# Five engines' orders, the PSUM banks, the load queues and the engines of copies dealt anew in a fused linear-attention and MLP kernel

## The chip, the cores and the metric

The kernel runs on one core of one Trainium2 chip. The metric is device time in microseconds (us), the median over several runs; lower is better. A run's time holds the span that the profile shows and some 3 us around it. The engines are PE (matmul; PEld is its weight load), DVE (VectorE), ACT (ScalarE), POOL (GpSimd) and SP, which here only issues transfers.

## The reference

```python
B, H, S, D = 4, 8, 768, 48                     # r, k, v, w: (B, H, S, D), f32
for t in range(S):                              # per batch and head, state (D, D)
    y[t] = r[t] @ (state + (u * k[t]) v[t]^T)
    state = w[t][:, None] * state + k[t] v[t]^T
x = y as (B*S, H*D) = (3072, 384)
h = x @ w_in                                    # (384, 1024)
solu = h * softmax(h)
ln = (solu - mean) / sqrt(var + 1e-6) * g_ln
out = ln @ w_out                                # (1024, 384)
```

## The kernel before

The sequence is cut into six chunks of 128 rows; with four batches that makes 24 units, `units = [(c, b) ...]`, of 128 rows and 384 columns each. Units of one batch follow each other through a state; units of different batches are free. Each unit goes through these stages, whose short names are the words of the order:

- Loads `LW LK LR LV` of w, k, r and v, 192 KB each, into rings of seven buffers (`NIO`). Weights come as `LI0..2` (w_in, 512 KB each), `LO0, LO1` (w_out, 768 KB each), `LU` and `LG`.
- Decays: `lw` (ACT, logarithm of w), `cum` (PE, running sums), `ex` (ACT, exponential in PSUM), `kp` (DVE, scaled k and r).
- Scores: `krk`, `krr` (PE transposes) with `kr` (a copy out of PSUM), or `kt` (a DMA transpose on SP in their place); `M` (PE) and `m` (masked copy, mostly DVE).
- The bonus of u: `p`, `q` (POOL products), `dg` (DVE sum), `vb` (v as bf16), `dv` (POOL).
- `Y` (PE, the output y) with `y` (copy), `S` (PE) with `et` (ACT) and `st` (DVE) for the next state. With `Y.i` the bonus is added by a matmul with the identity and `y` is a plain copy on ACT; with `Y.n`, `y` adds it on DVE.
- The MLP, transposed: `X` (PE) with `xT` (copy), `H` (PE, 24 matmuls of 128 columns, needs all of w_in), `e` (ACT, exp), `he` (DVE, product), `hq` (ACT, square), `ea` (POOL, halves the matmuls of a row sum), `Oa`, `Ob` (PE), `qm` (DVE), `lv`, `rs` (ACT), `o` (scaled copy) and `out` (store, through a ring of four buffers).
- Once: `wi` (cast of w_in), `gw` (w_out times gain), `mn` (PE column mean), `mc` (its copy, ACT), `ce` (centring of w_out), `hot` (warm-up matmuls on a tile of zeros; `hotN` has N of them).

No scheduler decides the order. A string, `ORDER`, lists some 900 words; each names a stage, a unit and, behind the dot, a choice. For PE words the choice is the PSUM bank, for copies the engine (`a` ACT, `d` DVE, `p` POOL), for loads and stores the queue:

```python
queue = {"": sp, "a": act, "g": pool}
...
for word in ORDER.split():
    word, _, how = word.partition(".")
    name = word.rstrip("0123456789")
    stages[name](int(word[len(name):]), how)
```

A wrapper, `InOrder`, keeps each engine's instructions in the order of the words, and SP's and ACT's transfers in one common order. An engine's queue is in order: an instruction that waits holds all behind it, a transfer's issue included. A transfer on SP or ACT also waits until the transfer eight places before it in the common order has landed, as both share eight semaphores in turn.

All of an engine's instructions come through the wrapper, so the profile gives nearly all of them the same line (L86), and groups are told apart by tile names: `ps` is any PSUM bank, `kr_in` the buffer of k and r, `w` (written `w<-`) the scaled w_out, `he`, `e`, `hq`, `o`, `y`, `st`, `et`, `xT`, `kr`, `kp`, `lw`, `vb`, `dv`, `dg` as above. ACTq and SPq rows are those engines' transfer issues.

Of the kernel before, what the change touches and what calls it, by code (L numbers as in the profile page):

```python
# [31 lines left out]
xT4.d ce1.d LK9 H2.6 hq0.a he1 e3 he3 LW12 e2 krk7.5 Oa0.2 he2 krr7 hq1.a cum10.3 LV8.g Ob0 ex10 Oa1.0 LR9 hq3.a
LV7 p8 cum8.6 LW13 Ob1 LW14 LK11 ex8 q7 vb6.p dg5 kr7.d kp10 lw11 qm0 Oa3.5 lv0 qm1 lv1 LV10.g p10 q8 rs0 M7.3
dg7 rs1 dv5 o0.a out0 vb7.p kp8 lw12 hq2.a Ob3 cum11.6 krk10.2 o1.d H4.0 m7.d Y5.n4 LR12.g dv7 Oa2.3 krr10 qm3
out1 p9 dg6 dg8 ex11 vb8.a dv6 q9 kp11 lv3 cum9.6 e4 rs3 Ob2 y5.d LV9 o3.a he4 ex9 kp9 lw14 kr10.a S7.5 LK12
Y6.n1 qm2 y6.d lv2 krk8.4 Y7.n0 krk11.6 krr8 y7.d S8.7 X5.2 et7 st7 krr11 lw13 rs2 LW17 o2.a et8 cum12.0 LR14.g
xT5.a ex12 q10 kr8.d S6.5 kr11.d hq4.a krk9.2 vb11.p out3 LK14 out2 M8.3 LK13 LR15.g LR17.g krr9 st8 kp12 LK17
et6 kr9.d H5.6 X6.0 m8.a M10.1 st6 e5 xT6.d M9.3 p11 Oa4.5 m10.d LW15 he5 q11 LR13.g X7.0 kt12 cum14.1 m9.a xT7.a
dv8 M11.3 ex14 m11.d sel8 Ob4 vb9.p kp14 LK15 hq5.a cum13.6 LW18 lw17 qm4 S11.0 ex13 Oa5.4 sel9 lv4 lw15 cum17.1
dg9 rs4 LR18.g kp13 Y8.n3 Ob5 ex17 cum15.6 y8.d dv9 o4.a Y9.n3 out4 LV12.g kp17 LV15.g et11 qm5 kt14 S9.5 st11  # L40
ex15 lv5 vb10.a y9.d H6.1 rs5 et9 LV14.g o5.a e6 st9 LV13.g kp15 p12 p13 dg11 he6 dg10 X8.3 X9.0 xT8.a H7.4 out5
q12 xT9.a e7 lw18 hq6.a H8.6 dv11 e8 M12.0 LV16.g he7 H9.2 m12.d LK18 Oa6.5 he8 dg12 e9 vb12.a S10.4 kt15 he9
hq7.a Ob6 hq8.a dv10 LW16 qm6 lv6 rs6 p14 LR16.g et10 Y11.n1 S12.0 et12 Oa7.6 o6.a LK16 y11.d lw16 Y10.n7 st10
Ob7 kt13 y10.d M14.3 st12 vb15.a LK20 M15.1 q13 vb13.a hq9.a qm7 m14.d m15.d lv7 dv12 rs7 Y12.n5 o7.a Oa8.0 y12.d
cum16.3 X11.7 Ob8 cum18.1 out6 p15 ex16 X12.5 xT11.d q14 q15 LR19.g qm8 kp16 vb16.a lv8 H11.6 rs8 o8.a ex18
xT12.d H12.4 LR20.g LW21 vb14.p dg13 LW19 dg15 e11 Oa9.0 p16 kp18 out7 e12 X10.1 dv15 he11 Ob9 xT10.a ea11.p he12
q16 lw21 hq11.a out8 qm9 lv9 M13.1 S15.3 et15 rs9 m13.d ea12.p cum21.4 ex21 o9.d H10.6 LK21 LR21 LW20 Oa11.0
LV18.g st15 kp21 lw19 cum19.1 e10 Ob11 Y15.n4 he10 hq12.a LK19 p18 kt16 S13.3 dv13 Y13.n5 S16.6 qm11 ex19 y15.d
lv11 out9 ea10.p kp19 LV22 LW22 rs11 et13 y13.d o11.a LK22 Oa12.7 out11 LV19.g lw20 M16.0 dg14 st13 vb18.a hq10.a
et16 m16.d p17 X15.4 Ob12 dv14 X13.3 p19 Y14.n2 xT15.d LR22 S14.5 xT13.d qm12 lv12 LV17.g rs12 st16 o12.a et14  # L50
kt17 y14.d q17 cum20.0 H13.3 dg16 H15.6 q18 ex20 st14 out12 e13 e15 vb19.a q19 kp20 he13 kt18 dv16 X14.2 xT14.d
Oa10.5 LV23 hq13.a Y16.n0 Ob10 dg17 he15 ea13.p qm10 lw22 vb17.a H14.1 ea15.p lv10 dv17 LW23 M17.6 y16.d kt19
dg18 rs10 Oa13.0 o10.a m17.d out10 cum22.3 X16.5 Ob13 e14 xT16.a Y17.n7 he14 qm13 dv18 kt20 p20 M18.5 vb23.p
y17.d hq15.a m18.d LV20.g ex22 kp22 H16.1 p21 LR23 Oa15.7 Y18.n6 dg19 dv19 LK23 q20 ea14.p p22 Ob15 X17.4 vb22.p
y18.d lv13 rs13 o13.a e16 hq14.a q21 X18.3 M19.5 he16 S18.0 vb20.p qm15 xT17.a m19.d ea16.p H17.1 dg20 dv20 out13
lv15 rs15 kt22 p23 kt21 et18 st18 o15.a lw23 M20.4 e17 Oa14.7 S17.0 xT18.a m20.d Ob14 hq16.a out15 cum23.5 he17
qm14 lv14 ex23 Y19.n3 rs14 q22 y19.d H18.1 dg21 LV21 vb21.p dv21 Y20.n4 o14.a kp23 Oa16.7 y20.d X19.3 et17 qh22
st17 X20.4 e18 Ob16 he18 ht17 xT20.a M21.5 xT19.a M22.3 qm16 m21.d hq17.a out14 lv16 H19.0 q23 Y21.n2 H20.5 m22.d
y21.d rs16 o16.a dg22 dv22 e19 X21.2 he19 kt23 dg23 hq18.a ht18 dv23 e20 xT21.d he20 Oa17.4 S19.7 hq19.a Y22.n3
Ob17 y22.d sv17 qm17 H21.1 out16 M23.5 et19 lv17 ht19 Oa18.3 ht20 st19 X22.0 e21 rs17 o17.a m23.d xT22.d Ob18  # L60
hq20.a Y23.n7 y23.d H22.4 sv18 qm18 lv18 xt23 he21 rs18 e22 Oa19.7 ea21.p o18.d Oa20.6 Ob19 out17 he22 hq21.a
# [606 lines left out]
```

## Time and profile before

| | |
|---|---|
| runs shown | 150.04, 149.55, 146.75 us; median 149.55 |
| profiled execution | 147.21 us, span 143.9 us, mean granted TensorE clock 0.975 |
| busy, share of the span | PE 90%, DVE 88%, ACT 83%, POOL 82% |
| chain that ended last | PE 56%, DMA 20%, DVE 11%, ACT 7% |
| transfers, share of 16 engines' span | SP's queue 66.2% (20.43 MB), POOL's 16.2% (6.49 MB), ACT's 10.2% (4.13 MB) |

A group's row has its line, engine, operation, tiles, shapes and count, then busy us and mean ns of one, then the idle time just before it and who ended it. Busy times of neighbours overlap a little, matmuls' a lot, so the step from one start to the next is the better price of a matmul.

### The profile page before, as it was taken

How to read it: one execution, taken by the hardware profiler on the slowest of the kernel's cores; microseconds unless marked ns; L12 is line 12 of the kernel's file. 1: busy time of each engine (PE TensorE's matmuls, PEld its weight loads, DVE VectorE, ACT ScalarE, POOL GpSimd, SP SyncE). 2: the span in 40 equal slices, each digit the busy share in tenths (PEclk: the TensorE clock that was granted, in tenths of full speed). 3: DMA queues.
4: the chain of work that ended last, by engine and by line, in shares of the span. 5: the costliest groups of instructions: out<-in, count | busy, mean ns of one | idle time of the engine just before them, and what ended most of it. 6: DMA issues, size and time to landing. Idle time of an engine off the chain costs nothing.

```text
span 143.9 us, 4779 instructions
## 1 busy us (share of the span) xinstructions
PE 129.1 (90%) x1883; PEld 96.4 (67%) x1883; DVE 126.3 (88%) x218; ACT 119.0 (83%) x241; POOL 117.7 (82%) x151
## 2 busy tenths in 40 slices
PE   6958749869599999999999999999999999999980
PEld 2326418657586778868988787779787565776750
DVE  6028998995899999999999999999999999989760
ACT  3547786989769999999998999959997979967762
POOL 7999959999999989978999999989996997433000
PEclk9995986999999999999999999999999999999999
DMA  4999999999998799999999999999999979443312
GB/s 95 276 287 323 272 310 356 365 348 261 179 267 185 133 245 247 240 201 178 256 225 257 239 262 222 194 280 228 199 199 226 204 170 140 116 107 118 135 55 109
DMA packets 89927, 31.33 MB, mean 218 GB/s; under 512 B 83833, under 2 KB 87938, under 8 KB 89906
## 3 DMA queue, kind: packets, MB, share of 16 engines
q1 hardware_dynamic: 77474, 20.43, 66.2%
q0 software_dynamic: 2112, 6.49, 16.2%
q10 hardware_dynamic: 10320, 4.13, 10.2%
q8 instruction: 14, 0.23, 0.6%
q14 instruction: 7, 0.06, 0.1%
HBM read 22.03 MB, written 4.72 MB: 186 GB/s over the span
## 4 chain that ended last, share of the span: by engine, by line
PE 56%; DMA 20%; DVE 11%; ACT 7%; issue 3%; DVEq 0%; ACTq 0%
PE ps L86 56%; DMA w_in<-in_w_dram 6%; DMA v_in<-in_v_dram 5%; DMA wout_f<-in_moe_w_out_dram 4%; DMA kr_in<-in_k_dram 4%; DVE kp L86 3%; DVE he L86 2%; DVE m L86 2%; ACT w L86 1%; DVE w L86 1%; ACT ps L86 1%; ACT lw L86 1%; DVE dg L86 1%; ACT o L86 1%; DVE y L86 1%
## 5 line engine op out<-in xcount | busy, mean ns | idle before, releaser
L86 PE MATMUL ps<-w,he 128*128 128x386 bf16 x192 | 43.7, 324 | 0.1
L86 PE MATMUL ps<-xT,win_sb 128*128 128x128 bf16 x480 | 29.8, 219 | 1.7 <-DVE kp L86 1.5
L86 PEld LDWEIGHTS <-win_sb 128*128 128x128 bf16 x480 | 27.4, 98 | 3.1 <-DVE kp L86 1.7
L86 DVE TENSOR_TENSOR kp<-ps,kr_in 128x768 bf16<-128x768 f32 x24 | 22.8, 949 | 7.3 <-DMA kr_in<-in_r_dram 4.2
L86 DVE TENSOR_TENSOR m<-ps,keep 128x1024 bf16<-128x1024 f32 x22 | 26.4, 1213 | 0.0
L86 PE MATMUL ps<-one_col,hq 128*128 128x1 bf16 x160 | 26.1, 163 | 0.1
L86 POOL TENSOR_TENSOR p<-kr_in 128x384 bf16<-128x384 f32 x24 | 24.1, 1009 | 1.9 <-DMA kr_in<-in_r_dram 1.7
L86 POOL TENSOR_TENSOR dv<-vb,dg 128x384 bf16<-128x384 bf16 x24 | 20.0, 833 | 6.6 <-DVE dg L86 6.5
L86 DVE TENSOR_TENSOR he<-ps,e 128x1024 bf16<-128x1024 f32 (+1 forms) x21 | 24.1, 1163 | 0.8 <-ACT e L86 0.8
L86 ACT ACTIVATE e<-ps 128x1024 bf16<-128x1024 f32 (+1 forms) x25 | 24.3, 989 | 0.2
L86 ACT ACTIVATE hq<-he 128x1024 bf16<-128x1024 bf16 (+1 forms) x20 | 20.5, 1033 | 2.3 <-DVE he L86 2.3
L86 POOL TENSOR_TENSOR q<-p,u_bc 128x384 bf16<-128x384 bf16 x24 | 21.7, 916 | 0.4 <-DVE dg L86 0.2
L86 PEld LDWEIGHTS <-he 128*128 128x128 bf16 x192 | 18.2, 96 | 3.8
L86 ACT ACTIVATE ps<-ps 128x768 f32<-128x768 f32 x24 | 19.1, 800 | 1.0 <-PE ps L86 0.7
L86 PEld LDWEIGHTS <-hq 128*128 128x128 bf16 x160 | 13.7, 96 | 8.5 <-ACT hq L86 0.3
L86 ACT ACTIVATE lw<-w_in 128x384 bf16<-128x384 f32 x24 | 12.4, 522 | 6.8 <-DMA w_in<-in_w_dram 6.8
L86 POOL DMA_DIRECT2D v_in<-in_v_dram x17 | 15.5, 912 | 0.0
L86 PEld LDWEIGHTS <-kp 128*128 128x128 bf16 x176 | 12.3, 105 | 4.3 <-DVE kp L86 2.7
L86 POOL DMA_DIRECT2D kr_in<-in_r_dram x16 | 14.7, 921 | 0.0
L86 PEld LDWEIGHTS <-kr 64*128 64x128 bf16 (+1 forms) x272 | 10.4, 95 | 6.1 <-issue 2.5
L86 PE MATMUL ps<-signs,e 128*128 128x2 bf16 x88 | 14.5, 165 | 0.0
L86 POOL TENSOR_TENSOR ea<-e 128x512 bf16<-128x512 bf16 x9 | 10.4, 1154 | 5.0 <-ACT e L86 5.0
(94 smaller groups left out, 281.1 us busy)
## 6 DMA issues: line engine op xcount, KB each, us to landing
out_dram<-o SPq DMA_DIRECT2D x24, 192.0 KB, 3.3
w_in<-in_w_dram SPq DMA_DIRECT2D x22, 192.0 KB, 4.7
kr_in<-in_k_dram SPq DMA_DIRECT2D x21, 192.0 KB, 4.5
v_in<-in_v_dram POOLq DMA_DIRECT2D x17, 192.0 KB, 4.8
kr_in<-in_r_dram POOLq DMA_DIRECT2D x16, 192.0 KB, 4.7
win_f<-in_moe_w_in_dram ACTq DMA_DIRECT2D x3, 512.0 KB, 6.6
kr_in<-in_r_dram SPq DMA_DIRECT2D x6, 192.0 KB, 3.9
v_in<-in_v_dram SPq DMA_DIRECT2D x5, 192.0 KB, 6.1
```

The costliest lines, as they stand in the source:

```text
L86: made = make(*args, **kwargs)
```

## The change

Only the string `ORDER` is replaced; every function stays. All words of work are there in both, with these choices counted:

| word | before | after |
|---|---|---|
| loads LW LK LR LV | SP 54, POOL 33, ACT 9 | SP 38, POOL 30, ACT 28 |
| LI, LO | ACT 4, SP 1 | ACT 3, SP 2 |
| stores `out` | SP 24 | SP 11, ACT 13 |
| `kr` copy | DVE 8, ACT 4 | DVE 4, ACT 7 |
| `kt` (DMA transpose) | 12 | 13 |
| `Y` | .n 20, .i 4 | .n 15, .i 9 |
| `y` | DVE 20, ACT 4 | DVE 15, ACT 9 |
| `xT` | ACT 12, DVE 11 | ACT 14, DVE 9 |
| `o` | ACT 18, DVE 6 | ACT 15, DVE 9 |
| `vb` | ACT 15, POOL 9 | ACT 8, POOL 10, DVE 6 |
| `ce` | DVE 6, POOL 2 | DVE 5, POOL 3 |
| `gw` | ACT 8 | ACT 7, DVE 1 |
| `ea` | 9 | 8 |
| `hot` matmuls | 15 | 24 |

Most words have other places than before, and most PE words other banks. The beginning, up to the first `Oa`, and the end:

```diff
-hot10.0 LK3.a LW3 LR3.g LW0.a LR0.a lw3 cum3.0 hot2.2 LU0 LW2 LK0.a LG0 lw0 LR2.g cum0.2 ex3 us0.4 LV0.a LW4 LK2
-lw2 lw4 kp3 gs0.5 ex0 LR4.g LK4 kp0 cum4.0 ih0 LV4.g ik0 LV2.g LV3.g LR6.g cum2.6 LW1.a uc0 p0 ex2 ex4 krk0.2 kp2
-krr0 krk3.4 LK1.a LW6 krk2.3 vb0.a krr2 LR5.g kr0.d kr2.a kp4 LK6 krr3 hot1.2 kr3.d M0.1 M3.3 m0.d LR1.a lw6 S0.0
-LV1.a m3.d p2 q0 lw1 gc0 LW5 cum6.6 ex6 M2.1 cum1.4 krk4.3 LI0.a krr4 LK5 dg0 m2.d vb3.a kp6 vb2.a lw5 et0 ex1
-st0 LO1 vb4.a kp1 cum5.6 hot1.0 q2 LV5.g p3 p1 dv0 ex5 krk1.4 q3 Y0.i5 q1 krr1 dg2 dv2 vb1.a krk6.0 S1.1 LO0.a
...
-S3.0 dv3 m1.d wi0.a M4.6 LW7 X0.1 xT0.d S2.5 gw7.a m4.d dg4 LV6.g et3 X2.4 p6 gw4.a LI1.a Y1.n1 LR7.g dv4 LR11.g
...
-st2 Y4.i5 st3 X1.0 lw7 LW9 xT2.a et5 y3.a st4 y4.a lw8 LK8 m5.d mn0.2 X3.4 xT1.d q5 cum7.0 xT3.a st5 ex7 p7 X4.5
-H0.6 lw10 mc0 ce7.p ce0.d e0 ce4.d LK10 ce6.d kp7 H1.3 LR8 ce2.d lw9 LW11 e1 he0 ce3.d LV11.g ce5.p H3.0 qh5
+LU0 LW0.a LW3 LR0.a hot5.1 LG0 LK0.a LW2 LW4 LR2.g us0.5 hot3.1 LK4 LK2.g hot2.1 lw0 hot6.0 LR3.g uc0 lw3 LK3.a
+LR4.g LW5 cum0.2 hot8.6 LV2.g ex0 lw2 LV0.a ih0 LK6 cum2.0 cum3.4 kp0 ex2 LV1.g lw4 LW1.a kp2 ex3 cum4.2 ik0 LW6
+krk0.7 ex4 p2 kp3 krr0 krk2.6 gs0.0 kr0.a LR1.a p0 krk3.5 kp4 krr2 krr3 LR5 q2 kr3.d M0.2 vb0.a LR6.g vb2.a m0.d
+krk4.5 S0.4 LV3.g et0 LK5 gc0 LK1.a dg2 M3.2 kr2.a krr4 q0 m3.d kr4.a LO0.a M2.0 LV4.g LO1 st0 lw1 p3 dg0 cum1.6
+LI2 m2.d lw6 LW7 dv2 ex1 cum6.4 vb1.d q3 lw5 kp1 ex6 cum5.2 LV5.g LW10 vb3.d ex5 S1.6 kp6 dv0 krk1.1 Y2.i7 et1
+vb4.a krr1 dg3 p1 S2.5 kr1.a krk6.4 st1 krr6 kp5 q1 Y0.i6 y2.a M1.0 LR10 et2 y0.a st2 dv3 kr6.a LI1.a dg1 S4.5
+m1.d dv1 X0.7 gw2.a M4.2 krk5.4 gw1.a LI0.a p4 m4.d krr5 gw3.a Y1.i6 et4 LW8.g M6.0 kr5.a xT0.d S3.3 st4 Y3.i7 q4
...
+wi2.p gw6.a X2.5 m5.d et5 wi0.a mn0.3 dv4 LR8 st5 lw7 LK10.a LR9.g xT2.d cum7.0 y4.d mc0 H0.6 xT3.a ce7.d LK8.g
+lw8 ce4.d ex7 LW11.a p5 ce6.d H1.4 e0 kp7 ce0.p LK12 lw10 he0 LK11 H3.0 ce3.p e1 LW9.a p6 ce1.d hq0.a H2.6 ce2.d
...
-EB23 out19 DA23 Ob21 QA23.a DB23 qm21 Ob22 lv21 rs21 QB23.d o21.a qm22 out20 out21 lv22 rs22 o22.d out22 Oa23.5
-Ob23 qm23 lv23 rs23 o23.a out23
+DA23 lv20 out17 rs20 Ob21 DB23 QA23.a out18.a o20.d Oa23.2 qm21 out20 QB23.d lv21 out19.a Ob22 rs21 o21.a Ob23
+qm22 lv22 rs22 o22.a out21.a qm23 lv23 rs23 o23.a out23.a
```

More of the change, by code (lines that the diff above doesn't have):

```diff
@@ L27 @@
-kp5 p5 p4 krr6 y0.a kr4.a dg3 krk5.5 dg1 dv1 q4 krr5 kr6.d kr1.a kr5.d et1 Y2.i6 hot1.0 y2.a vb5.a st1 LI2.a M1.2
-S3.0 dv3 m1.d wi0.a M4.6 LW7 X0.1 xT0.d S2.5 gw7.a m4.d dg4 LV6.g et3 X2.4 p6 gw4.a LI1.a Y1.n1 LR7.g dv4 LR11.g
-y1.d gw2.a gw5.a S4.2 LW10 M6.6 et2 et4 gw0.a S5.3 gw3.a LW8 wi2.p wi1.p gw1.a gw6.a LK7 Y3.i1 q6 m6.d M5.6 LR10
-st2 Y4.i5 st3 X1.0 lw7 LW9 xT2.a et5 y3.a st4 y4.a lw8 LK8 m5.d mn0.2 X3.4 xT1.d q5 cum7.0 xT3.a st5 ex7 p7 X4.5
-H0.6 lw10 mc0 ce7.p ce0.d e0 ce4.d LK10 ce6.d kp7 H1.3 LR8 ce2.d lw9 LW11 e1 he0 ce3.d LV11.g ce5.p H3.0 qh5
@@ L32 @@
[L32 to L61, printed above, removed]
@@ L62 @@
-Ob20 sv19 qm19 lv19 HA23.1 sv20 qm20 Oa21.0 rs19 HB23.3 lv20 out18 rs20 o19.d hq22.a o20.d ea22.p Oa22.7 EA23
-EB23 out19 DA23 Ob21 QA23.a DB23 qm21 Ob22 lv21 rs21 QB23.d o21.a qm22 out20 out21 lv22 rs22 o22.d out22 Oa23.5
-Ob23 qm23 lv23 rs23 o23.a out23
+LU0 LW0.a LW3 LR0.a hot5.1 LG0 LK0.a LW2 LW4 LR2.g us0.5 hot3.1 LK4 LK2.g hot2.1 lw0 hot6.0 LR3.g uc0 lw3 LK3.a
+LR4.g LW5 cum0.2 hot8.6 LV2.g ex0 lw2 LV0.a ih0 LK6 cum2.0 cum3.4 kp0 ex2 LV1.g lw4 LW1.a kp2 ex3 cum4.2 ik0 LW6
+krk0.7 ex4 p2 kp3 krr0 krk2.6 gs0.0 kr0.a LR1.a p0 krk3.5 kp4 krr2 krr3 LR5 q2 kr3.d M0.2 vb0.a LR6.g vb2.a m0.d
@@ new lines @@
+krk4.5 S0.4 LV3.g et0 LK5 gc0 LK1.a dg2 M3.2 kr2.a krr4 q0 m3.d kr4.a LO0.a M2.0 LV4.g LO1 st0 lw1 p3 dg0 cum1.6
+LI2 m2.d lw6 LW7 dv2 ex1 cum6.4 vb1.d q3 lw5 kp1 ex6 cum5.2 LV5.g LW10 vb3.d ex5 S1.6 kp6 dv0 krk1.1 Y2.i7 et1
+vb4.a krr1 dg3 p1 S2.5 kr1.a krk6.4 st1 krr6 kp5 q1 Y0.i6 y2.a M1.0 LR10 et2 y0.a st2 dv3 kr6.a LI1.a dg1 S4.5
+m1.d dv1 X0.7 gw2.a M4.2 krk5.4 gw1.a LI0.a p4 m4.d krr5 gw3.a Y1.i6 et4 LW8.g M6.0 kr5.a xT0.d S3.3 st4 Y3.i7 q4
+y1.a m6.d vb5.a X1.2 et3 LR7.g gw0.a dg4 y3.a S5.0 gw7.a wi1.p xT1.d M5.6 st3 X3.4 gw5.a LK7.a LW13 Y4.n2 gw4.d
@@ new lines @@
+wi2.p gw6.a X2.5 m5.d et5 wi0.a mn0.3 dv4 LR8 st5 lw7 LK10.a LR9.g xT2.d cum7.0 y4.d mc0 H0.6 xT3.a ce7.d LK8.g
+lw8 ce4.d ex7 LW11.a p5 ce6.d H1.4 e0 kp7 ce0.p LK12 lw10 he0 LK11 H3.0 ce3.p e1 LW9.a p6 ce1.d hq0.a H2.6 ce2.d
+q5 he1 e3 LV7.a LW17 Oa0.3 ce5.p e2 he3 LV8.a krk7.2 qh5 cum10.4 hq1.a LR12 LR11.g krr7 Ob0 he2 ex10 p7 Oa1.1 dg5
+lw13 qm0 LW12 kp10 hq3.a LV6.a cum8.6 q7 Ob1 vb7.d dv5 lv0 ex8 kr7.d Oa3.4 dg7 q6 hq2.a LV10.a LV11 Y5.i5 qm1 kp8
+p8 X4.2 rs0 Ob3 lv1 rs1 lw11 o0.d p10 xT4.a LK9.a cum11.6 o1.d y5.a M7.2 dg6 ex11 H4.0 dv7 m7.d lw9 LW14.a q8
@@ new lines @@
+X5.5 kp11 Oa2.3 e4 out0.a LV9.g vb8.d kt11 cum9.6 qm3 xT5.a vb6.p he4 Y7.n2 lv3 LR15.g Ob2 rs3 ex9 LK14 y7.d S7.1
+dv6 o3.a LR17 qm2 krk10.0 kp9 krk8.2 et7 lv2 p9 lw12 krr10 krr8 rs2 S8.5 st7 kr10.a LR13 p11 krk9.6 o2.d Y6.i4
+et8 lw14 kr8.d cum12.0 LW15.g y6.a krr9 st8 S6.2 ex12 kr9.d M8.4 q9 X6.3 hq4.a LR14.a dg8 H5.6 LW18.g kp12 et6
+m8.a LK17.a LK13.g xT6.d kt12 M10.0 st6 e5 M9.3 m10.d Oa4.5 sel8 out1 m9.a LK15 he5 dv8 X7.0 LV12 cum14.1 lw17
+LV15.a M11.3 sel9 ex14 Ob4 xT7.d m11.d hq5.a cum13.6 vb11.p LV13 Y8.i0 p12 qm4 lw15 kp14 Oa5.4 lv4 vb10.a q10 rs4
@@ new lines @@
+dg9 ex13 cum17.1 Ob5 o4.d vb9.p y8.a kp13 ex17 dv9 S11.3 S9.5 qm5 et11 LW21.g kp17 lv5 Y9.n0 rs5 et9 cum15.6 o5.a
+out4.a y9.d q12 H6.1 ex15 LR16.a st11 q11 st9 dg10 X9.0 X8.3 e6 LV17.g H7.4 kp15 xT8.a p13 dg11 kt15 lw18 H8.6
+he6 xT9.a dv11 e7 kt14 dg12 LW16.g M12.0 hq6.a he7 H9.2 LK18.g out2 vb12.a m12.d e8 out3.a p14 S10.4 Oa6.5 e9
+out5.a he8 dv12 LR21 Y11.n1 LR18 hq7.a Ob6 dv10 kt13 y11.d he9 q13 S12.0 et10 hq8.a Oa7.6 LK16.g st10 et12 hq9.a
+Y10.n1 st12 X11.4 vb13.p Ob7 qm6 xT11.a y10.d LV16 LK21.g vb15.a dg13 M14.3 lv6 M15.1 qm7 rs6 p15 LW19 Y12.n7
@@ new lines @@
+m14.d o6.a LV14.a Oa8.0 lv7 lw16 q14 rs7 y12.d o7.a cum16.3 m15.d Ob8 LK19 lw21 ex16 p16 cum18.6 X12.5 H11.1 kp16
+ex18 LW23.a q15 xT12.a qm8 LR19 vb14.p dg14 lv8 H12.4 rs8 p17 kp18 e11 kt16 dg15 p18 o8.a Oa9.3 he11 e12 X10.7
+S15.0 LK20 he12 ea12.p hq11.a Ob9 LV19 M13.1 et15 q17 xT10.a qm9 cum21.4 vb16.d lv9 m13.d H10.6 rs9 lw19 out7.a
+dv13 out8 ex21 LV21 dv15 st15 o9.a Y13.n2 kp21 cum19.0 e10 LW20.a q16 LR22 Oa11.3 y13.d ex19 ea10.p he10 S13.5
+Ob11 hq12.a kt17 LV22.g dg16 S16.2 et13 qm11 Oa12.6 kp19 lv11 dv14 rs11 et16 o11.a S14.7 st16 p19 kt19 X13.4 st13
@@ new lines @@
+M16.0 xT13.a Ob12 LK22.g m16.d hq10.a LR20.a kt18 LW22.a Y14.n5 q18 Y15.n4 qm12 y14.d H13.0 lv12 out6.a q19 y15.d
+et14 rs12 lw20 dg18 LV20 o12.a LV18.g X15.2 dg19 Oa10.5 e13 xT15.d st14 dv16 cum20.2 Ob10 he13 ex20 p20 H15.6
+kp20 ea13.p hq13.a qm10 kt20 X14.1 vb19.d M17.3 lv10 vb17.p rs10 xT14.d Y16.i0 e15 p22 m17.d H14.1 lw22 out11
+ea15.p y16.a he15 LR23 o10.a X16.4 Oa13.0 q22 e14 out9 xT16.d dg17 out12 Y17.n7 p21 hq15.a LK23.a kt21 he14
+cum22.3 M18.5 Ob13 vb18.p ex22 m18.d dv17 H16.1 dv18 kp22 dv19 Y18.n5 y17.d e16 kt22 S18.3 qm13 ea14.p X17.6
@@ new lines @@
+y18.d Oa15.7 lv13 xT17.a he16 out10 et18 rs13 M19.4 LV23.g lw23 Ob15 hq14.a m19.d q21 H17.1 vb22.a o13.d qh22
+hq16.a vb20.p qm15 M20.4 st18 lv15 q20 Oa14.0 e17 m20.d ea16.p Y19.i3 rs15 o15.a he17 X18.6 cum23.4 xT18.a Ob14
+vb21.p y19.a p23 dg20 ex23 S17.6 qm14 H18.2 lv14 dv20 kp23 rs14 et17 o14.a out13.a st17 kt23 Y20.n1 e18 dg21
+Oa16.7 y20.d dv21 X19.5 ht17 X20.6 he18 Ob16 xT19.a vb23.p q23 M21.4 qm16 M22.2 hq18.a ht18 m21.d H19.0 xT20.a
+m22.d lv16 Y21.n4 rs16 o16.a H20.5 e19 out14.a y21.d dg23 X21.7 dg22 S19.2 e20 he19 dv22 Oa17.4 Y22.n3 dv23 et19
@@ new lines @@
+xT21.a he20 Ob17 ht19 hq17.a H21.0 y22.d ht20 hq19.a st19 sv17 M23.6 sv18 Oa18.5 qm17 hq20.a m23.d X22.2 Ob18
+lv17 out15.a sv19 e21 xT22.d Y23.n6 H22.2 y23.d qm18 xt23 he21 Oa19.7 e22 Oa20.6 out16 lv18 he22 ea22.p Ob19 rs18
+hq21.a Ob20 ea21.p qm19 HA23.0 sv20 lv19 rs19 hq22.a o19.d HB23.3 o18.d Oa21.7 rs17 EA23 qm20 o17.d EB23 Oa22.1
+DA23 lv20 out17 rs20 Ob21 DB23 QA23.a out18.a o20.d Oa23.2 qm21 out20 QB23.d lv21 out19.a Ob22 rs21 o21.a Ob23
+qm22 lv22 rs22 o22.a out21.a qm23 lv23 out22 rs23 o23.a out23.a
```

## The prediction

> **What bounds the kernel now.** I read the busy time by stage first, because the page's shares (PE 90%, DVE 88%, ACT 83%, POOL 82%) mix a start, a long middle and a tail.
>
> The view of stages. Columns: stretch, its length, then for each engine busy us (instructions), granted TensorE clock, DMA share, GB/s.
> ```profile
> 4.00:16.00 12.00, 9.41 (x67) 5.20 (x66) 5.78 (x7) 6.82 (x11) 11.56 (x21) 0.86 1.20 291
> 16.00:36.00 20.00, 15.46 (x225) 11.28 (x224) 17.36 (x26) 17.48 (x40) 18.25 (x21) 0.91 1.13 324
> 36.00:40.00 4.00, 2.48 (x45) 2.31 (x43) 3.56 (x6) 2.65 (x5) 3.98 (x6) 1.00 0.91 179
> 40.00:70.00 30.00, 29.62 (x489) 23.63 (x487) 30.00 (x49) 28.75 (x56) 27.54 (x34) 1.00 0.95 216
> 70.00:100.00 30.00, 29.99 (x520) 24.80 (x518) 29.86 (x48) 27.64 (x57) 29.27 (x33) 1.00 1.09 236
> 100.00:126.00 26.00, 25.88 (x376) 18.31 (x374) 25.90 (x39) 23.68 (x50) 21.62 (x27) 1.00 0.93 184
> 126.00:143.90 17.90, 13.54 (x175) 9.85 (x172) 11.63 (x26) 10.72 (x26) 2.31 (x2) 0.99 0.33 104
> ```
> From 40 to 126 us both PE (85.5 of 86) and DVE (85.8 of 86) are full. ACT leaves 1.25 + 2.36 + 2.32 = 5.9 us in those 86, so nothing but less PE **and** less DVE work shortens the middle, while a modest burden on ACT lengthens it. The start is different: up to 36 us the DMA engines are full (share over 1) and the compute engines are not.
>
> What holds the start, from the chain that ended last (start us, us, what):
> ```profile
> 16.16 6.83 DMA v_in<-in_v_dram
> ...
> 23.01 0.01 ACT vb L86
> 23.02 6.20 DMA wout_f<-in_moe_w_out_dram
> ```
> ACT sat in front of `vb1` until 22.99; only then did it issue half of w_out (23.02), which landed at 29.22. The rows where that comes out, from the timelines of POOL, PE, ACT and DVE:
> ```profile
> 32.62 2.03 POOL L86 CAST win_sb<-win_f 128x1024 bf16<-128x1024 f32 x2
> 34.49 3.02 PE L86 MATMUL ps<-xT,win_sb 128*128 128x128 bf16 x48
> 35.90 0.51 ACT L86 CAST mean_sb<-ps 128x384 bf16<-128x384 f32 x1
> 36.44 1.67 DVE L86 SCALAR_TENSOR_TENSOR w<-wout_f,gr,ps 128x384 bf16<-128x384 f32 x3 [2.13 <-ACT mean_sb L86]
> 39.41 1.22 DVE L86 TENSOR_TENSOR he<-ps,e 128x1024 bf16<-128x1024 f32 x1
> ```
> The last w_in slice is cast at 32.62, `H0` starts at 34.49, the column mean is copied at 35.90, DVE stands for 2.13 us waiting for it, and `he0` comes at 39.41. From there on two engines are full.
>
> **The change part by part.** I counted words of both orders and compared the built instruction lists. No function changes, only which engine, bank, queue and place each step gets.
>
> *1. Engines of copies.* Rows that carry the prices (busy us, mean ns of one):
> ```profile
> L86 DVE TENSOR_TENSOR y<-ps,dv 128x384 bf16<-128x384 f32 x20 | 10.9, 548 | 0.5 <-PE ps L86 0.4
> L86 DVE COPY kr<-ps 128x1024 bf16<-128x1024 bf16 x8 | 5.3, 680 | 0.6 <-PE ps L86 0.6
> L86 DVE COPY xT<-ps 128x384 bf16<-128x384 bf16 x11 | 3.7, 346 | 0.0
> L86 DVE TENSOR_SCALAR o<-ps,rs 128x384 f32<-128x384 f32 x6 | 3.6, 610 | 0.6 <-ACT rs L86 0.6
> L86 DVE SCALAR_TENSOR_TENSOR w<-wout_f,gr,ps 128x384 bf16<-128x384 f32 x6 | 3.5, 608 | 2.1 <-ACT mean_sb L86 2.1
> L86 ACT COPY kr<-ps 128x1024 bf16<-128x1024 bf16 x4 | 4.0, 1016 | 0.9 <-PE ps L86 0.9
> L86 ACT CAST y<-ps 128x384 bf16<-128x384 f32 x4 | 1.9, 494 | 0.0
> L86 ACT COPY xT<-ps 128x384 bf16<-128x384 bf16 x12 | 5.6, 481 | 0.5 <-PE ps L86 0.3
> L86 ACT ACTIVATE o<-ps,rs 128x384 f32<-128x384 f32 x18 | 10.4, 579 | 0.4
> L86 ACT CAST vb<-v_in 128x384 bf16<-128x384 f32 x15 | 7.4, 508 | 1.4 <-DMA v_in<-in_v_dram 1.4
> L86 ACT ACTIVATE w<-wout_f,gr 128x384 bf16<-128x384 f32 x8 | 4.5, 618 | 0.6 <-DMA wout_f<-in_moe_w_out_dram 0.6
> ```
> DVE: kr 8 to 4 (-2.72), y 20 to 15 (-2.74), xT 11 to 9 (-0.69), o 6 to 9 (+1.83), one `ce` less and one `gw` more (0), and six `vb` casts that DVE does not do in this trace. Their price lies between the xT copy (0.35) and the f32 scaling `o` (0.61), for the same 384 columns; I take 0.48, the middle, since they read f32 like the one and only copy like the other: +2.9, ends +2.1 and +3.7. Sum -1.4 us (ends -2.2 and -0.6). ACT: kr 4 to 7 (+3.05), y 4 to 9 (+2.47), xT 12 to 14 (+0.96), o 18 to 15 (-1.74), vb 15 to 8 (-3.56), gw -0.62: +0.6 us.
>
> *2. POOL.* Thirty DMA issues instead of 33 at 0.92 (-2.75), one vb more (+0.51), one `ce` more (+0.84), one `ea` less (-1.15): -2.6 us. POOL is not full in any stretch after 100 us and its loads lead; worth 0. It hides behind PE and DVE; should DVE become the shorter one, it is 2.6 us of cover, no cost.
>
> *3. PE.* Five more y sums start with a matmul of `dv` against the identity, 384 columns; back to back such a matmul takes 0.17 us, as the two starts show:
> ```profile
> 33.99 0.33 PE L86 MATMUL ps<-lw,uti_neg 128*128 128x384 bf16 x1
> 34.16 0.33 PE L86 MATMUL ps<-lw,uts 128*128 128x384 bf16 x1
> ```
> so +0.83. Unit 11's kr goes through the DMA transpose, minus eight transposes of 128 columns at 3.02 / 48 = 0.063: -0.5. One `ea` less is four small matmuls more, +0.1. Net +0.4. Nine more warm-up matmuls (24 for 15) stand before the first `ex` results; PE waits for data there (9.41 of 12 busy, warm-ups included), so 0; without that cover nine times 512 columns at 0.17 per 384 are 2.0 us, and twice that at half the clock.
>
> The middle is bounded by the larger of PE (+0.4) and DVE (-1.4, half of it in the start, where three of the kr copies stood, so -0.7). Ends -0.7 and +0.4; I take **-0.2**, between them, since both engines are full.
>
> *4. ACT's queue.* It carries 28 loads, three weight loads and 13 stores, where it carried 9 loads and four weight loads, all before 27 us. What an issue costs ACT, and what it costs when a queue is behind, from the timelines of ACT and SP; the last row, of the DMA issues, ends with the us from issue to landing:
> ```profile
> 11.31 0.80 ACT L86 ACTIVATE ps<-ps 128x768 f32<-128x768 f32 x1
> 11.32 0.46 ACTq L86 DMA_DIRECT2D kr_in<-in_k_dram  x1
> 12.02 0.79 ACT L86 ACTIVATE ps<-ps 128x768 f32<-128x768 f32 x1
> ...
> 90.99 0.40 SPq L86 DMA_DIRECT2D v_in<-in_v_dram  x1
> 91.44 0.73 SPq L86 DMA_DIRECT2D w_in<-in_w_dram  x1
> 92.26 2.29 SPq L86 DMA_DIRECT2D kr_in<-in_k_dram  x1
> 94.63 0.86 SPq L86 DMA_DIRECT2D out_dram<-o  x1
> ...
> kr_in<-in_k_dram SPq DMA_DIRECT2D x21, 192.0 KB, 4.5
> ```
> ACT's issue of 0.46 runs under the exponential before it: 11.31 to 12.02 is 0.71, no longer than the step without an issue. So a clear issue costs 0 behind an instruction of 0.4 us or more, and in the new list nearly all of ACT's issues stand behind such a one (an `e`, `hq`, `ex`, `lw` or copy); the exceptions, behind `gr`, `lv` or another issue, are seven. But the fourth load in a row on SP held that sequencer for 2.29 us. SP did nothing else; on ACT the same hold stops the next activation, and behind it DVE's `he` and PE's `Oa`. By word order and PE work between, ACT's queue has two, at most three, transfers under way, SP's had three to four (its loads land after 4.5 us, and its 98 issues come one per 1.5 us of the span). Each hardware transfer also waits for the one eight before it; the smallest spacing on ACT behind `H0` is 5.8 us of PE work (`LW22`), against 4.5 to land. Some 25 of ACT's issues lie in the 86 full us. Lower end 0. Upper end: each as dear as those four on SP, mean 1.07, of which 0.4 is covered: 25 x 0.67 = 16.8, less ACT's 5.9 idle = +10.9, with no gain below 0 since an issue gives ACT nothing. The rows of ACT itself are nearer; I take **+0.8** (seven uncovered of 0.3 and two short holds, most absorbed in the 5.9).
>
> The Trainium skill, "DMA: Bandwidth & Descriptors", section "Anatomy of one DMA — SWDGE (gpsimd) path", speaks against the change here: a DMA engine waits for no semaphore, the wait stands on the issuing sequencer. The trace agrees for ACT in front of `vb1`, where 23.02 follows 22.99. By that rule every lane wait and buffer wait of a moved load becomes ACT's own.
>
> *5. The start.* `LO0` now stands behind `kr4` and ahead of `lw1`; `vb1` moves to DVE. That cuts the link 16.16 to 23.02: my estimate is an issue near 17 to 18, after the first four `kp`. But the start is full of bytes: counting words, 8.65 MB precede the end of the last w_in slice before, 8.84 MB after; at 324 GB/s that is 0.6 us later, not earlier. What is gained is order: the column mean is copied right ahead of `H0`, so DVE's 2.13 idle should halve, and `he0` has one `ce` fewer ahead of it (0.6). Together -1.1 - 0.6 + 0.6 = **-1.1**, ends -4 (rival C) and +2 (`K1` stands 1.2 MB later in the order, 3.6 us at 324 GB/s, and so `kp1`; other units' work covers part).
>
> *6. The tail.* The last `o` and its store now share ACT; `out21` is issued between `o22` and `lv23`:
> ```profile
> 140.03 0.20 ACT L86 ACTIVATE lv<-qm 128x1 f32<-128x1 f32 x1 [1.10 <-DVE qm L86]
> 140.26 0.20 ACT L86 ACTIVATE rs<-lv 128x1 f32<-128x1 f32 x1
> 140.50 0.58 ACT L86 ACTIVATE o<-ps,rs 128x384 f32<-128x384 f32 x1
> ```
> ACT stood idle 1.10 there; `o22` (0.58) and an issue fill it but for **+0.2** (0 to 0.5).
>
> **Sum**: -0.2 + 0.8 - 1.1 + 0.2 = -0.3. The profiled execution took 147.21 (span 143.9, 3.3 around it), so 146.9. The three runs shown have 146.75, 149.55 and 150.04: the profiled one stands 2.3 under their median. A new median may fall on either level, so I add about half, 1.1: **148.0**.
>
> **The rivals.**
>
> *B, ACT is held (slower).* Place: ACT's issues between 40 and 126 us. For: SP's 2.29 row, and a middle with two full engines. Against: ACT's own issue at 0.46, and the spacing of 5.8 us and more. Price: if the mean hold is 0.85 instead of 0.46, 25 x 0.45 = 11.2, less 5.9 = +5.3. It decides once the holds exceed those 5.9 us. Then 147.21 - 0.2 - 1.1 + 0.2 + 5.3 = 151.4, with the 1.1 of the forecast 152.5; and more if stores come late, since `o` then waits for its buffer (4 to 17 us of PE work from a store to the next use in the middle, 7 to 22 before).
>
> *C, the start gets faster.* For: the chain through `vb1` and w_out is cut, and two hardware queues share the loads. The page shows that the DMA engines did more when larger packets came:
> ```profile
> GB/s 95 276 287 323 272 310 356 365 348 261 179 267 185 133 245 247 240 201 178 256 225 257 239 262 222 194 280 228 199 199 226 204 170 140 116 107 118 135 55 109
> ```
> At 350 GB/s from 4 us on, 8.5 MB need 24.3 us and `H0` starts 4 us sooner: 147.21 - 4 - 0.2 + 0.2 (ACT) + 0.2 (tail) = 143.4, with the 1.1 it is 144.5. Against: the share was already 1.13 to 1.20, and small packets remain.
>
> The Trainium skill, same page, section "Issuing engines are not separate DMA queues", says that starting DMAs on several engines saves only issue time, since all share the 16 DMA engines. By it C fails and the time stays that of the sum.
>
> *D, nothing moves.* The full engines hide it all: the sum's ends cancel. That is the forecast itself within its spread of 2 us.
>
> **How the numbers follow.** Forecast (with D) 0.48, B 0.30, C 0.22. Own range of the forecast 145.5 to 150.5. To leave out no more than 2 in 10 the range reaches to C at 144.0 and past B to 153.5. Some 2% is what a measurement of this kernel can tell from no change (its three runs differ by 2.2%). B gives slower, except for 0.02 of it; C gives faster: 0.22 faster, 0.50 same, 0.28 slower.
>
> **What would show it.** Right: PE and DVE full from some 39 us on; ACT's idle in the middle near 4 us; ACTq rows of 0.35 to 0.6; first `he` at 38 to 39 us; six DVE casts at 0.35 to 0.61. Wrong towards B: ACTq rows over 1 us, and PE or DVE waiting for ACT's `e` or `hq` behind them. Wrong towards C: `H0` at 31. Wrong altogether: a clock below 1.00 in the middle, or `o` waiting for stores.

## The result and the profile after

The changed kernel takes **156.62 us** (median of 156.85, 156.61, 156.63 and 155.77); the kernel before, beside it on the same chip, 148.15. The ratio is **1.067, 95% interval 1.060 to 1.073**: slower, by more than the forecast's range allowed (153.5). The profiled execution took 156.85 with a span of 155.1, against 143.9 before: 11.2 us more, of which 9.6 show in the time (156.85 against 147.21), since 1.8 us lie around this span and 3.3 lay around the one before. Ratios here and below compare only executions within 1.5% of their kernel's fastest: of "all three undone" these are three of ten (146.87 to 147.57, the others 151.19 to 158.34); beside the four kernels without a ratio the kernel before had only one of six (145.27, the others 149.21 to 152.47); and the profiles of four kernels (prompt stores, K1 early, loads on SP, POOL's and SP's letters) are of executions 1.5 to 2% above the fastest.

The view of stages of the changed kernel, columns as in the prediction (stretch, length, busy us of PE, PEld, DVE, ACT, POOL, granted clock, DMA share, GB/s):

```profile
4.00:16.00 12.00, 10.63 (x54) 4.72 (x53) 3.74 (x4) 5.99 (x11) 11.58 (x21) 1.00 1.21 285
16.00:36.00 20.00, 12.10 (x181) 9.11 (x181) 15.06 (x22) 13.70 (x29) 12.19 (x14) 0.74 0.97 290
36.00:40.00 4.00, 2.95 (x43) 1.87 (x40) 4.00 (x5) 3.23 (x7) 4.00 (x6) 1.00 0.70 154
40.00:70.00 30.00, 28.76 (x456) 22.84 (x456) 30.00 (x48) 28.02 (x53) 28.22 (x33) 1.00 1.03 209
70.00:100.00 30.00, 27.66 (x471) 22.88 (x470) 27.76 (x42) 26.40 (x53) 25.27 (x31) 1.00 1.15 206
100.00:126.00 26.00, 24.89 (x395) 18.81 (x394) 24.69 (x39) 20.45 (x44) 24.91 (x30) 1.00 1.07 202
126.00:155.00 29.00, 23.18 (x297) 16.43 (x297) 21.57 (x38) 19.87 (x48) 6.38 (x8) 0.96 0.51 125
```

From 16 to 36 us PE is busy 12.1 us where it was 15.5, and the DMA share, 1.13 before, is 0.97 (290 GB/s for 324): the start waits, and even the DMA engines do less. From 70 to 126 no engine is full any more: PE 52.6 of 56, DVE 52.5, ACT 46.9, POOL 50.2.

I follow the delay by three marks that both kernels have: the first `he`, the last `lv`, the end.

| us | before | after | more |
|---|---|---|---|
| start of the first `he` | 39.4 | 43.9 | +4.5 |
| first `he` to last `lv`, length | 100.6 | 106.0 | +5.4 |
| last `lv` to end of span, length | 3.9 | 5.2 | +1.3 |

**The start.** Timelines of PE, ACT, DVE and POOL; the bracket is the idle time before the instruction, and who ended it:

```profile
3.54 0.52 ACT L86 ACTIVATE lw<-w_in 128x384 bf16<-128x384 f32 x1 [1.46 <-DMA w_in<-in_w_dram]
5.07 4.71 PE L86 MATMUL ps<-warm 128*128 128x512 bf16 x11
9.62 0.33 PE L86 MATMUL ps<-lw,uti_neg 128*128 128x384 bf16 x1
9.95 1.89 PE L86 MATMUL ps<-warm 128*128 128x512 bf16 x8
17.51 0.18 ACT L86 ACTIVATE et<-ps 128x8 f32<-128x8 f32 x1 [0.94 <-PE ps L86]
17.52 0.37 ACTq L86 DMA_DIRECT2D kr_in<-in_k_dram  x1
25.98 0.96 DVE L86 TENSOR_TENSOR kp<-ps,kr_in 128x768 bf16<-128x768 f32 x1 [4.07 <-DMA kr_in<-in_k_dram]
30.67 0.35 ACTq L86 DMA_DIRECT2D win_f<-in_moe_w_in_dram  x1
```

`lw0` is done at 4.06, yet `cum0` runs at 9.62, behind eleven warm-up matmuls. `K1` is issued at 17.52, right behind the first `et`, for which ACT had waited; before, it was issued at 11.32. It lands at 25.90 where it landed at 17.64: 6.2 us by the later issue, 2.1 by a longer time from issue to landing (8.4 us, not 6.3). DVE stands 4.07 us in front of `kp1`. The last two loads of w_in leave at 30.67 and 31.12; before, at 25.37 and 26.70.

The granted clock from 16 to 36 us is 0.74 where it was 0.91; the same running-sum matmul of 384 columns that takes 0.33 us at 9.79 takes 0.53 at 20.61. The granted clock there is 0.83 with K1 early and 1.00 with all three parts undone (both below). How much of the 4.5 us is the clock's, no run separates.

**The middle and the tail.** Timelines of SP and ACT:

```profile
75.76 3.94 SPq L86 DMA_TRANSPOSE kr<-kp  x2
79.75 0.57 SPq L86 DMA_DIRECT2D out_dram<-o  x1
82.03 7.85 SPq L86 DMA_TRANSPOSE kr<-kp  x1
87.20 0.58 ACT L86 ACTIVATE o<-ps,rs 128x384 f32<-128x384 f32 x1 [2.16 <-DMA out_dram<-o]
103.36 1.14 ACTq L86 DMA_DIRECT2D w_in<-in_w_dram  x1
104.74 1.40 ACTq L86 DMA_DIRECT2D out_dram<-o  x1
147.50 0.34 ACTq L86 DMA_DIRECT2D out_dram<-o  x1
151.44 0.58 ACT L86 ACTIVATE o<-ps,rs 128x384 f32<-128x384 f32 x1 [1.11 <-DMA out_dram<-o]
```

`out2` is issued at 79.75, 23 us later than before (56.5): its word stands later, and there behind two DMA transposes on SP. It frees the buffer that `o6` needs, so ACT stands 2.16 us. At the end `o23` stands for `out19` (147.50), 1.11 us more than it need. Of ACT's issues behind `H0` only two are held (1.14 and 1.40 us).

**DVE's new copies.** Groups of DVE (busy us, mean ns of one, idle before):

```profile
L86 DVE CAST vb<-v_in 128x384 bf16<-128x384 f32 x6 | 4.5, 751 | 0.0
L86 DVE TENSOR_SCALAR w<-wout_f,gr 128x384 bf16<-128x384 f32 x1 | 2.4, 2359 | 0.0
```

The six casts cost 0.75 each, not 0.48, and the one scaling of w_out 2.36, not 0.61.

### The profile page after: what moved, and what is told of

Same layout as the page of the kernel before. It is cut to its first block, busy times and chain, and to the rows that moved or that the text cites. A ratio compares the mean times of both kernels' runs of the same rounds, so it can differ in the third digit from the quotient of the medians.

```text
span 155.1 us, 4783 instructions
## 1 busy us (share of the span) xinstructions
PE 132.9 (86%) x1890; PEld 97.7 (63%) x1893; DVE 129.0 (83%) x216; ACT 119.4 (77%) x240; POOL 115.7 (75%) x149
## 4 chain that ended last, share of the span: by engine, by line
PE 36%; POOL 18%; DMA 17%; DVE 13%; issue 9%; ACT 6%; DVEq 0%; ACTq 0%; POOLq 0%
PE ps L86 35%; DMA kr_in<-in_r_dram 6%; DMA kr_in<-in_k_dram 5%; POOL p L86 5%; POOL q L86 4%; DVE kp L86 3%; DMA w_in<-in_w_dram 2%; DMA out_dram<-o 2%; DVE he L86 2%; POOL kr_in L86 2%; POOL dv L86 2%; ACT e L86 2%; DVE m L86 2%; POOL m L86 1%; DVE dg L86 1%
## 5 line engine op out<-in xcount | busy, mean ns | idle before, releaser
L86 PE MATMUL ps<-w,he 128*128 128x386 bf16 x192 | 43.5, 325 | 0.1
L86 PE MATMUL ps<-signs,e 128*128 128x2 bf16 x96 | 15.8, 165 | 0.0
L86 POOL TENSOR_TENSOR ea<-e 128x512 bf16<-128x512 bf16 x8 | 9.2, 1154 | 6.9 <-ACT e L86 6.9
L86 PEld LDWEIGHTS <-kp 128*128 128x128 bf16 x168 | 11.2, 102 | 2.6 <-DVE kp L86 0.5
L86 DVE TENSOR_REDUCE dg<-q 128x8 f32<-128x384 bf16 (+1 forms) x24 | 12.5, 523 | 0.2 <-POOL q L86 0.2
L86 PE MATMUL ps<-kr 64*128 64x128 bf16 x192 | 9.2, 218 | 2.9 <-DMA kr<-kp 1.7
```

The source lines that it names most:

```text
L86: made = make(*args, **kwargs)
```

## The experiments

The theory before the runs, L: the loss is a late start, stores late behind their `o`, and dear DVE casts. The rival, Q: ACT carries too many transfers as such (the forecast's rival B). In these kernels the helper's line is L84. Times are medians beside the kernel before on the same chip; the marks are read from the timelines of DVE and ACT as above.

| kernel | median us | ratio to before (95%) | first `he` | last `lv` | span |
|---|---|---|---|---|---|
| stores prompt | 153.58 | 1.031 (1.018 to 1.045) | 43.6 | 148.2 | 152.3 |
| queues back to SP | 156.32 | 1.053 (1.041 to 1.066) | 44.4 | 150.0 | 155.0 |
| start of after, rest of before | 153.21 | 1.037 (1.029 to 1.044) | 46.2 | 147.0 | 151.1 |
| start of before, rest of after | 152.68 | 1.035 (1.026 to 1.045) | 38.1 | 145.9 | 150.3 |
| casts back | 154.38 | none | 42.6 | 148.3 | 153.7 |
| fewer warm-ups | 154.02 | none | 43.5 | 148.1 | 152.3 |
| fewer warm-ups, K1 early | 152.34 | none | 39.8 | 146.9 | 151.1 |
| start of before, rest with stores and casts undone | 149.12 | none | 39.0 | 141.6 | 145.6 |
| all three undone in the changed order | 153.52 | 1.007 (0.998 to 1.016) | 39.2 | 141.0 | 145.2 |
| rest with stores and casts undone, loads on SP | 153.01 | 1.031 (1.024 to 1.039) | 38.5 | 147.0 | 151.2 |
| before, all new queue letters | 151.32 | 1.036 (1.028 to 1.045) | 40.2 | 145.6 | 149.6 |
| splice of both | 147.25 | 1.003 (0.997 to 1.009) | 38.6 | 141.1 | 145.3 |
| before, only ACT's letters | 148.58 | 1.010 (1.002 to 1.019) | 39.5 | 143.0 | 147.3 |
| before, only POOL's and SP's letters | 150.25 | 1.016 (1.005 to 1.028) | 39.1 | 145.3 | 149.3 |

**Stores prompt.** Each store right behind its `o`, on SP:

```diff
-... H9.2 LK18.g out2 vb12.a m12.d e8 out3.a p14 ...
+... o3.a out3 LR17 ... o2.d out2 Y6.i4 ...
```

> The changed kernel with every store placed right behind its o and on SP, as the kernel before has them; all loads stay where the change put them. Theory L (the loss is a late start, 4.5 us, stores issued 0.8 to 18 us after their o, so that later o's wait for a buffer, 3.5 us, and dearer DVE casts, 1.5 us): 153 us, the waits of o for a store of 3.3, 2 and 2.2 us gone. Theory Q (ACT carries too many transfers as such, wherever they stand): most loads are still on ACT, so 155.5 to 156.6.

153.6, as theory L said. `out2` is issued at 61.6, and `o6`'s row (ACT's timeline) has no wait:

```profile
84.97 0.58 ACT L84 ACTIVATE o<-ps,rs 128x384 f32<-128x384 f32 x1
```

The last `lv` comes 1.7 us earlier and the end follows it after 4.1 us in place of 5.2. Moving 13 stores also takes 13 issues from ACT. The next run takes them away, too, at the late places, and gains next to nothing; prompt stores that stay on ACT were not tried in the changed order.

**Queues back to SP.** All of ACT's loads and stores behind `H0` on SP, at the same words:

```diff
-... LW11.a ... out0.a ... LW22.a ... out6.a ...
+... LW11   ... out0   ... LW22   ... out6   ...
```

> The changed kernel with all of ACT's loads and stores behind H0 given to SP, at the same places of the order. Theory L: the two held issues near 103 to 106 us go, the late stores stay late: 155.0 to 156.5. Theory Q: ACT is free of its issues from 44 us on, so the loss behind the start goes: 151 to 152.

156.3: next to nothing gained. ACT's two held issues are gone, and the loss stays. Late stores still make `o` wait, but 1.1 us in all (0.17 at `o6`, 0.93 at `o23`), so this run doesn't fit theory L cleanly either. Theory Q's 151 to 152 is missed; but SP now carries ACT's loads as well, and a run below shows that this can cost time of its own, so the run alone doesn't clear ACT's issues. The run with all three parts undone, where ACT keeps its 28 loads, says more.

**Two splices**, at `H0`: the start of one kernel with the rest of the other (words in the order of the kernel they come from; at the joint the first has two words on other banks, the second `X4` at a later place).

> The changed order up to H0, and behind it the remaining words of the order before, in their order. Theory L: only the later start is left of the loss, 148.2 + 4.5 = 152.7. If the start's delay is soaked up by slack behind it: 148 to 149. Theory Q: ACT's loads behind H0 are gone, so 148 to 150.

> The order before up to H0, and behind it the remaining words of the changed order. Theory L: the start is back, 156.6 - 4.5 = 152.1. If the start was soaked up anyway, or theory Q holds alone: 156 to 157.

153.2 and 152.7, both within 0.6 us of theory L. About half of the loss is made before `H0` and half behind it. With the start of after and the rest of before, first `he` to last `lv` takes 100.8 us (before 100.6): the delay of the start isn't soaked up by anything. Its first `he` comes at 46.2, though, 2.3 us later than in the changed kernel, as the order before has other words between `H0` and `he0`; so that the time agrees with theory L to 0.5 us is partly luck.

**Casts back.** `vb1 vb3 vb8 vb16 vb19 gw4` back to ACT and `vb7` to POOL:

```diff
-vb1.d vb3.d gw4.d vb7.d vb8.d vb16.d vb19.d
+vb1.a vb3.a gw4.a vb7.p vb8.a vb16.a vb19.a
```

> The changed kernel with the six v casts and the one scaling of w_out that the change gave to DVE back on the engines that had them before (ACT and POOL). Theory L (DVE pays for these far more than the 0.48 and 0.61 forecast while POOL works; 4.5 + 2.4 us in the trace): 154 to 155, the column mean some 1 us earlier. Rival (the casts hide in DVE's slack, and on ACT and POOL they cost as much): 156 to 157.5.

154.4. The column mean is copied at 39.49 in place of 40.15 and the first `he` starts 1.3 us earlier; the last `lv` 1.6 earlier. So most of that price seems to be the one scaling `gw4`, for which PE's column mean waited: the two casts ahead of it took only 0.35 each. Behind the first `he` the casts are worth 0.3.

**Fewer warm-ups, and K1 early.**

```diff
-... lw0 hot6.0 LR3.g ... cum0.2 hot8.6 LV2.g ... cum2.0 ... lw4 LW1.a ... et0 LK5 gc0 LK1.a
+... lw0 LR3.g ... cum0.2 LV2.g ... cum2.0 ... lw4 LK1.a LW1.a ... et0 LK5 gc0
```

The first run has the two `hot` words taken out, the second that and `LK1.a` moved.

> The changed kernel without the two groups of 6 and 8 warm-up matmuls that stand on PE just before and just behind cum0 (the other ten stay). Theory L: cum0 runs at 7 us in place of 9.6, all behind it some 2 us earlier: 154 to 155. Rival M (the start is bound by bytes, and PE waits for data there): 156 to 157. Rival K (without them PE's granted clock is lower for some us): 157 to 158.

> As the run without the two groups of warm-ups, and the load K1 issued on ACT right ahead of W1 in place of behind et0, four words of ACT earlier. Theory L: kp1 at some 20 to 21 us instead of 26, so 152 to 153. Rival M (bytes bind the start, an earlier K1 only delays others): no faster than without the warm-ups, 155 to 157.

The first median, 154.0, is what theory L said, but for a reason it had not: `kp0` comes 2.1 us earlier (8.9), `kp1` still at 25.5, and the first `he` only 0.4 earlier. K1 was issued 1.7 us earlier (15.78) and landed only 0.45 earlier, 9.7 us after its issue. The warm-ups cost the start next to nothing while K1 is late. Without them the running sums at 7.2 us take 0.53 each, as rival K would have it, but the time is not longer. The rest of the gain in time lies at 82 to 87 us, where SP's transpose took 3.45 us in place of 7.85, `out2` was issued at 77.99, and `o6` did not wait. That wait is on a knife's edge: with K1 early it is back, at 2.49 us. K1 is the start's price: issued at 10.18 it lands at 15.56 and brings `kp1` to 20.73 and the first `he` to 39.8. DVE's timeline of that second run:

```profile
8.89 0.96 DVE L84 TENSOR_TENSOR kp<-ps,kr_in 128x768 bf16<-128x768 f32 x1 [5.79 <-ACT ps L84]
...
20.73 0.96 DVE L84 TENSOR_TENSOR kp<-ps,kr_in 128x768 bf16<-128x768 f32 x1 [0.16 <-ACT lw L84]
```

The bytes allow it, so rival M falls: an earlier K1 does not just delay others.

**Stores and casts undone behind the start of before; then all three undone in the changed order.**

> The order before up to H0, behind it the remaining words of the changed order, with the stores right behind their o on SP and the DVE casts back on ACT and POOL. ACT still carries its loads. Theory L: 152.7 as measured with the start of before, less 3 for the stores as measured alone and 0.5 to 1.5 for the casts: 148 to 149.5. Rival (other parts of the new order cost, too: banks, places of PE words, loads on ACT): 150.5 to 152.

> The changed order with the three edits together: K1 issued earlier and without the two groups of warm-ups, stores right behind their o on SP, the DVE casts back on ACT and POOL. All else (orders, banks, the other copies, ACT's 28 loads) is as changed. Theory L (start, stores and casts are the loss): first he at 38 to 39.5, total 148 to 149.5. If one of the three only seemed to matter: 151 or more.

149.1, and 1.007 of the kernel before (three of its ten executions), an interval that holds 1. In the second, every other part of the change is in place: orders, banks, kr and y copies, ACT's 28 loads. Its stages:

```profile
16.00:36.00 20.00, 16.31 (x210) 11.84 (x210) 17.28 (x26) 17.21 (x36) 15.92 (x19) 1.00 1.10 317
36.00:40.00 4.00, 3.68 (x63) 3.55 (x63) 3.52 (x6) 3.96 (x8) 3.98 (x5) 1.00 0.86 190
40.00:70.00 30.00, 30.00 (x490) 23.71 (x488) 29.77 (x48) 28.74 (x57) 29.71 (x37) 1.00 1.14 243
70.00:100.00 30.00, 29.50 (x508) 23.90 (x505) 28.82 (x45) 27.56 (x57) 27.56 (x32) 1.00 1.15 235
100.00:126.00 26.00, 26.00 (x382) 18.45 (x381) 25.17 (x36) 22.72 (x49) 21.02 (x27) 1.00 0.94 165
```

PE is full again (85.5 of 86), as before. **The three parts are nearly all of the loss**: the span is 145.2 us, 9.9 of the 11.2 are gone, and the interval leaves at most 1.6%. Between first `he` and last `lv` 2.0 us are left in the first run (102.6 for 100.6) and 1.2 in the second, and what they are stays open. Behind the first `he`, prompt stores alone win 1.4 us and casts alone 0.3, both together 3.4 (102.6 against 106.0). That with one stall gone the other ends last would explain it; it isn't shown, and the profile of prompt stores is one of the four named above, so 1.4 may be too low.

**Loads of ACT to SP in the mended rest.**

> The order before up to H0, the remaining words of the changed order with stores prompt and casts back, and now the loads of ACT behind H0 on SP as well, at the same places. In the trace without this last edit 2.0 us of loss were left between the first he and the last lv. Theory Q (ACT's issues cost them): 1 to 2 us below the run without the edit, 146.5 to 148. Theory O (places and banks of the words cost them): no change, 148.5 to 149.5; an SP that holds its loads: up to 151.

Slower, 1.031: neither theory's number, though the last clause named it. SP's and DVE's timelines:

```profile
100.47 1.27 SPq L84 DMA_TRANSPOSE kr<-kp  x1
101.79 0.57 SPq L84 DMA_DIRECT2D kr_in<-in_r_dram  x1
105.89 0.96 DVE L84 TENSOR_TENSOR kp<-ps,kr_in 128x768 bf16<-128x768 f32 x1 [3.32 <-DMA kr_in<-in_r_dram]
```

`R20`, issued by ACT at 95.3 in the run without this edit, now stands behind SP's DMA transposes until 101.79, and DVE waits 3.32 us. ACT's queue was the better place for it. Whether ACT's loads are part of the 2.0 us left, this run therefore cannot say.

**The queue letters alone, on the order before**; then split into those that lead to ACT (30) and the other 24:

```diff
-out0 ... out6 ... LW22 ... LK21   LV16.g ...
+out0.a ... out6.a ... LW22.a ... LK21.g LV16 ...
```

> The kernel before with nothing changed but the queue letters behind H0: each load and store goes to the queue that the change gave it (13 stores and 17 loads on ACT), at its old place, stores right behind their o. Theory L: the queues as such cost 0 to 1 us, 148 to 149 where the kernel before takes 148. Theory Q and the forecast's rival B: 151 to 153.

> The kernel before with only those queue letters behind H0 changed that lead to ACT: 13 stores and 17 loads, at their old places. All else as before. Theory P (what the queue letters cost is one K load, of unit 21, that POOL now issues behind its products): 147 to 148.5, no change. Theory Q (ACT's issues cost it): 150.5 to 151.5.

> The kernel before with only the other queue letters behind H0 changed: 10 loads from SP to POOL and 14 from POOL to SP, at their old places. Theory P: 150.5 to 151.5, DVE's kp of unit 21 waiting some 2.6 us for its k. Theory Q: 147 to 148.5, no change.

All letters give 1.036 and 151.3 us: against theory L's expectation, and the number that theory Q and rival B had. The split shows that ACT is not the whole of it: ACT's 30 alone give 1.010 (1.002 to 1.019) and 148.6, not Q's 150.5 to 151.5; the other 24 give 1.016 (1.005 to 1.028). In the last, POOL's and DVE's timelines:

```profile
89.47 1.17 POOL L84 TENSOR_TENSOR ea<-e 128x512 bf16<-128x512 bf16 x1
90.56 0.92 POOL L84 DMA_DIRECT2D kr_in<-in_k_dram  x1
94.76 0.96 DVE L84 TENSOR_TENSOR kp<-ps,kr_in 128x768 bf16<-128x768 f32 x1 [2.77 <-ACT ps L84]
```

`K21`, on SP at 84.3 before, is issued by POOL at 90.56, behind its products and sums, and `kp21` starts 0.1 us after it landed; DVE stands 2.77 us. So the queue letters do cost something in an order that was not made for them, through one late load on POOL and through ACT's letters; which costs more, the two intervals don't tell. In the changed order POOL issues the same load at 83.6, and this wait isn't there.

**A splice of both** (start of before, the mended words to the `he` of unit 5, then the order before):

> The order before up to H0, then the changed words (stores prompt, casts back) up to the he of unit 5, which came there 0.8 us earlier than in the kernel before, then the remaining words of the order before. If that lead is kept: 0.5 to 1 us below the kernel before. If the joint loses it: the same time.

1.003: the same time. At the `he` of unit 9 the lead is a lag of 1.0 (76.7 against 75.7): the joint lost it. No run beats the kernel before.

## Why the prediction was wrong, point by point

- **Step 5, the start, failed**: forecast -1.1, measured +4.5. It weighed K1's place by bytes (1.2 MB later, "other units' work covers part"). Its issue is set by the queue: it stands behind `et0`, so behind `kp0`, `S0` and PE. That is 6.2 of the 8.3 us by which it landed later (11.32 to 17.52), and the order of ACT's words shows the wait; the other 2.1 are the longer time from issue to landing, which the queue's order does not explain (with fewer warm-ups, too, a K1 issued 1.7 us earlier landed only 0.45 earlier). The cover was not there either: `kp6`, `kp5` and POOL's products stand behind `kp1` in their queues. The run with K1 early took 3.7 of the 4.1 us off that were left without the warm-ups. The estimate for `LO0` (17 to 18) came out at 18.70, but w_out was no longer what the start waited for.
- **Step 1, DVE, failed in size and sign**: forecast -1.4, and DVE's busy time went from 126.3 to 129.0. I priced casts from f32 SBUF by copies and scalings out of PSUM, a different source: 0.75 us each in place of 0.48, the scaling 2.36 in place of 0.61. Undoing them brought the last `lv` 1.6 us earlier.
- **Steps 4 and 6 left the stores' places out of the sum.** Rival B had the words ("more if stores come late"), with distances counted in PE work, and the last section listed "`o` waiting for stores" as what would make it wrong; no term stood for it. With prompt stores the last `lv` comes 1.7 us earlier and the end follows it 1.1 sooner.
- **Step 4's own term was near right.** ACT's issues took 0.34 to 0.6 but for three (0.75 in the start, 1.14, 1.40), and the letters that lead to ACT cost 1.0% in the order before (0.2 to 1.9%), some 1.5 us for the 0.8 taken. Giving ACT's transfers behind `H0` to SP won next to nothing. Rival B's mechanism, long holds, is thus not what happened, though its side was. "By that rule every lane wait and buffer wait of a moved load becomes ACT's own": true, but what counted more is the reverse, that ACT's own waits became the load's, as at K1.
- **Step 3**: the nine more warm-ups, priced 0, delayed `kp0` but are worth 0.4 at the first `he`. The zero held, not for the reason given (PE did not wait for data there, `lw0` was done at 4.06) but because K1 came later still.
- **Step 2**: POOL's busy time fell by 2.0 us (117.7 to 115.7) where 2.6 were forecast; what that is worth was not tried by itself.
- **Rival C** failed: two queues did not fill the DMA engines, whose share from 16 to 36 us fell to 0.97; with K1 early it is 1.10.

## What to carry to other kernels

Where a transfer is moved to a compute engine's queue, read what that engine waits for just ahead of the new place, and price the transfer's lateness before its issue cost. Give each store's place a term of its own: from its landing to the next use of its buffer. A copy moved between engines is priced by a row with the same source memory, and by what the engine beside it does meanwhile.
